# Loads and DMA transposes of an attention-plus-MLP kernel taken two pairs at a time and held apart

## The chip, the cores and the metric

One NeuronCore of a Trainium2 chip. The metric is the device time of one execution in microseconds (us), the median of several; most executions of the kernel before agree within 0.3%. A profile is one execution; its span is some 1.7 to 2.8 us shorter than the time of the same execution, since the time includes what lies before the first and after the last instruction.

## The reference, cut to what matters

```python
# q, k, v: (4 batches, 8 heads, 768 steps, 64) float32
for t in range(S):
    state = gamma * state + outer(k_t, v_t)          # per batch and head
    y_t   = scale * q_t @ state
x = y as (3072 tokens, 512)
h = x @ w_in                                         # 512 -> 2048
out = (h * cos(h)) @ w_out                           # 2048 -> 512
```

The kernel does the recurrence in chunks of 128 steps. A **pair** is one chunk of two batches: its q, k, v are 6 x 256 KB, and there are 12 pairs (0 to 11). A **group** is two pairs, 512 tokens of the MLP. "The fourth pair" is pair 3.

## The kernel before: the parts that matter

For every pair: load q, k, v (DMA); multiply q and v by decay factors and turn them into bf16 (`conv_q`, `conv_v`, mostly on POOL); turn k into bf16 (`conv_k`, on ACT); transpose q and k (`stage_t` on PE with an eviction by DVE, or `stage_t_dma`, a DMA transpose from SP); scores on PE and masking on DVE (`attend`); output and state (`stage_y`), whose result ACT copies into `xt`, the MLP's input. The MLP's first half is `unit_f` / `pair_f` (matmuls, cosine on ACT, product on DVE), its second half `unit_o`.

In these profiles each engine takes its instructions in the order in which the program emits them, and stands at the first one that isn't ready (below, ACT stands 2.33 us at the conversion of k5 with cosines behind it). POOL issues the loads, too. The stretch around pairs 3 to 6, cut:

```python
conv_k(3, True)                                      # ACT
conv_q(3, nc.gpsimd)                                 # POOL
load(nc.sync, 4, ("q0", "q1"))                       # SP issues, 256 KB each
load(nc.gpsimd, 4, ("k0", "k1", "v0", "v1"))         # POOL issues
conv_v(3, nc.gpsimd)
load(nc.sync, 5, ...); load(nc.gpsimd, 5, ...)
...
pair_f(2, 0)
stage_t(3, 0); stage_t(3, 1)                         # PE: 16 transposes, DVE: 2 evictions
pair_f(2, 1)
attend(3)
conv_q(4, nc.gpsimd); conv_v(4, nc.gpsimd); conv_k(4, True)
stage_t_dma(4)                                       # SP: DMA transposes, two a pair
load(nc.gpsimd, 6, ...)
pair_f(2, 2); pair_f(2, 3, (0,))
stage_y(3, nc.scalar.copy)                           # writes xt, which pair_f(3, .) reads
pair_f(2, 3, (1,))
conv_q(5, ...); conv_v(5, ...); load(nc.gpsimd, 7, ...)
pair_f(3, 0)
conv_k(5, True); stage_t_dma(5)
...
```

So loads of later pairs and transposes of earlier ones are in flight side by side. Source buffers are reused (`SLOT`), converted tiles have three copies (`NB = 3`).

## Time and profile before

| | before |
|---|---|
| time, median of 4 runs | 208.88 us (208.86 to 209.13) |
| span of the profiled run (a further one, of 209.35 us) | 207.6 us |
| PE busy | 199.5 us, 96% |
| POOL busy | 102.3 us, 49% (99.8% from 50 to 110 us) |
| DMA transposes, issue to landing | 2.7 / 4.6 / 13.8 us (least, median, most) |

The prediction shows how the page is read. Two more stretches of the timeline matter for what follows (columns: start, length, engine, line, what, count). POOL, which issues a load of 256 KB about every 0.88 us:

```profile
54.84 0.93 POOL L132 DMA_DIRECT2D qf<-in_q_dram  x1
55.77 0.88 POOL L132 DMA_DIRECT2D kf<-in_k_dram  x1
56.65 0.88 POOL L132 DMA_DIRECT2D qf<-in_q_dram  x1
57.52 0.88 POOL L132 DMA_DIRECT2D kf<-in_k_dram  x1
```

### The profile page before, as it was taken

How to read it: one execution, taken by the hardware profiler on the slowest of the kernel's cores; microseconds unless marked ns; L12 is line 12 of the kernel's file. 1: busy time of each engine (PE TensorE's matmuls, PEld its weight loads, DVE VectorE, ACT ScalarE, POOL GpSimd, SP SyncE). 2: the span in 40 equal slices, each digit the busy share in tenths (PEclk: the TensorE clock that was granted, in tenths of full speed). 3: DMA queues.
4: the chain of work that ended last, by engine and by line, in shares of the span. 5: the costliest groups of instructions: out<-in, count | busy, mean ns of one | idle time of the engine just before them, and what ended most of it. 6: DMA issues, size and time to landing. Idle time of an engine off the chain costs nothing.

```text
span 207.6 us, 4155 instructions
## 1 busy us (share of the span) xinstructions
PE 199.5 (96%) x1624; PEld 113.5 (55%) x1646; DVE 113.3 (55%) x188; ACT 114.1 (55%) x193; POOL 102.3 (49%) x118
## 2 busy tenths in 40 slices
PE   6889999999999999999999999999999999999993
PEld 1467554558997555546544465544465444444452
DVE  4691984554957454869874466854367244443000
ACT  6767872257996336577753754653554653553120
POOL 8999238399999999999995230000000000000000
PEclk9999999999999999999999999999999999999999
DMA  6999999999999999959799931141101100110222
GB/s 158 351 237 203 215 252 287 336 261 358 258 251 257 264 252 254 255 184 218 242 177 92 252 82 50 55 103 51 51 3 51 51 18 36 51 52 21 80 77 78
DMA packets 36644, 33.83 MB, mean 163 GB/s; under 512 B 26768, under 2 KB 29072, under 8 KB 36624
## 3 DMA queue, kind: packets, MB, share of 16 engines
q0 software_dynamic: 7808, 20.98, 39.4%
q1 hardware_dynamic: 27632, 12.23, 25.4%
q10 hardware_dynamic: 1184, 0.36, 0.7%
q8 instruction: 13, 0.21, 0.4%
q14 instruction: 7, 0.06, 0.1%
HBM read 27.26 MB, written 6.29 MB: 162 GB/s over the span
## 4 chain that ended last, share of the span: by engine, by line
PE 91%; DVE 4%; DMA 2%; issue 1%; DVEq 0%
PE bank L381 38%; PE bank L340 32%; PE bank L351 7%; PE bank L281 3%; PE bank L259 3%; PE bank L286 2%; DMA qf<-in_q_dram 2%; DVE am L268 2%; PE bank L398 2%; PE bank L232 1%; PE st_ps L303 1%; DVE qk L197 1%; DVE qkt L216 1%; PE bank L362 1%; PE bank L369 1%
## 5 line engine op out<-in xcount | busy, mean ns | idle before, releaser
L333 DVE TENSOR_TENSOR gt<-bank,cosb 128x512 bf16<-128x512 f32 x96 | 64.9, 689 | 61.9 <-ACT cosb L329 61.4
L329 ACT ACTIVATE cosb<-bank,halfpi 128x512 bf16<-128x512 f32 x96 | 65.1, 688 | 50.0 <-PE bank L340 44.4
L381 PE MATMUL bank<-w_out_sb,gt 128*128 128x512 bf16 x359 | 88.5, 379 | 0.7 <-issue 0.3
L340 PE MATMUL bank<-xt,w_in 128*128 128x512 bf16 x294 | 74.3, 380 | 0.7 <-issue 0.3
L381 PEld LDWEIGHTS <-gt 128*128 128x128 bf16 x368 | 35.5, 98 | 41.2
L340 PEld LDWEIGHTS <-w_in 128*128 128x128 bf16 x304 | 33.7, 114 | 30.9
L268 DVE TENSOR_TENSOR am<-bank,mask 128x512 bf16<-128x512 f32 x48 | 30.4, 682 | 3.9 <-PE bank L259 3.9
L388 ACT COPY ob<-bank 128x512 f32<-128x512 f32 x23 | 13.4, 586 | 18.4 <-PE bank L381 18.4
L204 POOL TENSOR_TENSOR vs<-vf,gk 128x512 bf16<-128x512 f32 x21 | 21.4, 1045 | 2.9 <-PE st_ps L303 2.9
L132 POOL DMA_DIRECT2D vf<-in_v_dram x23 | 20.3, 885 | 4.8 <-DMA w_out_sb<-in_moe_w_out_dram 4.8
L197 POOL TENSOR_TENSOR qk<-qf,gq 128x512 bf16<-128x512 f32 x18 | 18.5, 1051 | 7.8 <-issue 4.9
L132 POOL DMA_DIRECT2D kf<-in_k_dram x21 | 18.9, 901 | 1.8 <-DMA w_out_sb<-in_moe_w_out_dram 1.6
L210 ACT CAST qk<-kf 128x512 bf16<-128x512 f32 x24 | 13.9, 615 | 9.3 <-DMA kf<-in_k_dram 9.3
L290 ACT CAST xt<-bank 128x512 bf16<-128x512 f32 x24 | 12.9, 589 | 6.7 <-PE bank L286 6.7
L132 POOL DMA_DIRECT2D qf<-in_q_dram x18 | 16.2, 902 | 0.8 <-DMA w_in<-in_moe_w_in_dram 0.8
L351 PE MATMUL bank<-xt,w_in 128*128 128x256 bf16 x128 | 14.7, 273 | 0.0
L351 PEld LDWEIGHTS <-w_in 128*128 128x128 bf16 x128 | 13.8, 114 | 0.4
L286 PE MATMUL bank<-am,vs 128*64 128x128 bf16 x192 | 11.6, 220 | 0.0
L281 PEld LDWEIGHTS <-stb 128*64 128x64 bf16 x160 | 8.7, 109 | 4.3 <-issue 3.8
L281 PE MATMUL bank<-qkt,stb 128*64 128x128 bf16 x160 | 10.7, 222 | 0.3 <-DVE am L268 0.3
L286 PEld LDWEIGHTS <-vs 128*64 128x64 bf16 x192 | 9.9, 110 | 0.5 <-issue 0.4
L315 DVE CAST stb<-st_ps 64x512 bf16<-64x512 f32 x12 | 8.2, 685 | 2.7 <-PE st_ps L303 2.6
(46 smaller groups left out, 86.8 us busy)
## 6 DMA issues: line engine op xcount, KB each, us to landing
vf<-in_v_dram POOLq DMA_DIRECT2D x23, 256.0 KB, 5.8
out_dram<-ob SPq DMA_DIRECT2D x23, 256.0 KB, 2.0
kf<-in_k_dram POOLq DMA_DIRECT2D x21, 256.0 KB, 5.7
qf<-in_q_dram POOLq DMA_DIRECT2D x18, 256.0 KB, 5.3
w_out_sb<-in_moe_w_out_dram POOLq DMA_DIRECT2D x4, 512.0 KB, 12.5
qf<-in_q_dram SPq DMA_DIRECT2D x6, 256.0 KB, 8.1
w_in<-in_moe_w_in_dram POOLq DMA_DIRECT2D x3, 512.0 KB, 8.1
kf<-in_k_dram POOLq DMA_DIRECT2D x1, 512.0 KB, 5.4
```

The lines of the kernel that those rows point to most:

```text
L132: eng.dma_start(out=t[SLOT[p]][b], in_=src[2 * bp + b, :, ds(c * C, C)].rearrange("h t d -> t h d"))
L197: eng.tensor_tensor(out=qk[p % NB][:, b, 0], in0=qf[SLOT[p]][b], in1=bc(gq, p % NC), op=ALU.mult)
L204: eng.tensor_tensor(out=vs[p % NB][:, b], in0=vf[SLOT[p]][b], in1=bc(gk, p % NC), op=ALU.mult)
L210: nc.scalar.copy(out=qk[p % NB][:, b, 1], in_=kf[SLOT[p]][b])
L268: nc.vector.tensor_tensor(out=am[p % 2][b][j], in0=ap[j], in1=mask.unsqueeze(1).to_broadcast([128, HP, 128]), op=ALU.mult)
L281: nc.tensor.matmul(yp[ts(j, 64), a, :], lhsT=stb[p % 2][:, b, a, ts(j, 64)], rhs=qt(n, b, a), start=True, stop=False, skip_group_check=True)
L286: nc.tensor.matmul(yp[ts(j, 64), a, :], lhsT=vs[n][:, b, 2 * a + j, :], rhs=am[p % 2][b][j][:, a, :], start=(c == 0), stop=True, skip_grou ...
L329: nc.scalar.activation(out=cb, in_=bank, func=AF.Sin, bias=halfpi)
L333: nc.vector.tensor_tensor(out=out, in0=bank, in1=cb, op=ALU.mult)
L340: nc.tensor.matmul(bank, lhsT=w_in_t(i, f), rhs=xt[g % 2][:, i, :], start=(i == 0), stop=(i == KIN - 1))
L351: nc.tensor.matmul(bank[:, ts(e, 256)], lhsT=w_in_t(i, f + e), rhs=xt[g % 2][:, i, ts(hf, 256)], start=(i == 0 and e == 0), stop=(i == KIN ...
L381: nc.tensor.matmul(bank, lhsT=gt[g % 2][:, f, ts(j, 128)], rhs=w_out_sb[:, f, :], start=(f == 0), stop=(f == KOUT - 1))
```

## The change

The intent: take the fourth pair's transposes off PE, and from that pair on let the DMA do one kind of thing at a time, for two pairs: six loads of 512 KB (both batches in one transfer), then the transposes of both pairs. What holds the next loads back is a **gate**, a small copy on POOL that reads what the first of the last pair's two transposes writes: POOL can't issue the next loads before that one has landed. The core of the diff:

```diff
-    def load_k(p): ...
+    def load_both(*names):
+        for n, p in names:                       # one 512 KB transfer, both batches
+            bp, c = divmod(p, NC)
+            nc.gpsimd.dma_start(out=both[n][SLOT[p]]..., in_=SRC[n][1][2 * bp : 2 * bp + 2, ...])
...
+            conv_k(3, True)
-    conv_k(3, True)
-    conv_q(3, nc.gpsimd)
-    load(nc.sync, 4, ...) ; load(nc.gpsimd, 4, ...) ; conv_v(3, nc.gpsimd)
-    load(nc.sync, 5, ...) ; load(nc.gpsimd, 5, ...)
+    def turn(ps, loads=()):
+        for p in ps: conv_q(p, nc.gpsimd)
+        for p in sorted(ps): stage_t_dma(p)
+        for p in sorted(ps): conv_v(p, nc.gpsimd)
+        if loads:
+            nc.gpsimd.tensor_copy(out=gate, in_=qkt[max(ps) % NB][:, 0, 1, HP - 1, 126:])
+            load_both(k, q of the first, k, q of the second, v, v)
+    turn((3,), (4, 5))
...
     pair_f(2, 0)
-    stage_t(3, 0)
-    stage_t(3, 1)
+    conv_k(4, True)
     pair_f(2, 1)
     attend(3)
-    conv_q(4, ...) ; conv_v(4, ...) ; conv_k(4, True) ; stage_t_dma(4) ; load(nc.gpsimd, 6, ...)
+    conv_k(5, True)
+    turn((5, 4), (6, 7))
...  # the same for later pairs: turn((6, 7), (8, 9)), turn((8, 9), (10, 11)), turn((10,)), turn((11,))
```

`conv_k(4)` and `conv_k(5)` move forward on ACT, and the q product of pair 5 comes before that of pair 4. The conversions of later k are moved as well.

More of the change, by code (lines that the diff above doesn't have):

```diff
@@ L97 @@
     w_out_sb = sb([128, KOUT, DM], BF16, "w_out_sb")
-    qf = [[sb([128, H, D], FP32, f"qf{i}_{b}") for b in range(2)] for i in range(PRE)]
-    kf2 = [sb([128, 2, H, D], FP32, f"kf{i}") for i in range(PRE)]
-    kf = [[t[:, b] for b in range(2)] for t in kf2]
-    vf = [[sb([128, H, D], FP32, f"vf{i}_{b}") for b in range(2)] for i in range(PRE)]
+    both = {n: [sb([128, 2, H, D], FP32, f"{n}f{i}") for i in range(PRE)] for n in "qkv"}
+    qf, kf, vf = [[[t[:, b] for b in range(2)] for t in both[n]] for n in "qkv"]
     ob = [sb([128, DM], FP32, f"ob{i}") for i in range(4)]
@@ L120 @@
     rel = sb([128, 128], FP32, "rel")
+    gate = sb([128, 2], BF16, "gate")
     SRC = {"q": (qf, q), "k": (kf, k), "v": (vf, v)}
@@ L134, in load @@
                 in_=src[2 * bp + b, :, ds(c * C, C)].rearrange("h t d -> t h d"))
-    def load_k(p):
-        bp, c = divmod(p, NC)
-        nc.gpsimd.dma_start(
-            out=kf2[SLOT[p]].rearrange("p b h d -> p (b h) d"),
-            in_=k[2 * bp : 2 * bp + 2, :, ds(c * C, C)].rearrange("b h t d -> t (b h) d"))
+    def load_both(*names):
+        for n, p in names:
+            bp, c = divmod(p, NC)
+            nc.gpsimd.dma_start(
+                out=both[n][SLOT[p]].rearrange("p b h d -> p (b h) d"),
+                in_=SRC[n][1][2 * bp : 2 * bp + 2, :, ds(c * C, C)].rearrange(
+                    "b h t d -> t (b h) d"))
     def load_w_in(r):
@@ L171 @@
     load(nc.gpsimd, 1, ("q1",))
-    load_k(1)
+    load_both(("k", 1))
     load(nc.gpsimd, 0, ("v0", "v1"))
@@ L493 @@
             conv_v(2, nc.vector, (1,))
+            conv_k(3, True)
         elif u == 11:
             stage_m(2, stage_a(2, 1))
-    conv_k(3, True)
-    conv_q(3, nc.gpsimd)
-    load(nc.sync, 4, ("q0", "q1"))
-    load(nc.gpsimd, 4, ("k0", "k1", "v0", "v1"))
-    conv_v(3, nc.gpsimd)
-    load(nc.sync, 5, ("q0", "q1", "v0"))
-    load(nc.gpsimd, 5, ("k0", "k1", "v1"))
+    def turn(ps, loads=()):
+        for p in ps:
+            conv_q(p, nc.gpsimd)
+        for p in sorted(ps):
+            stage_t_dma(p)
+        for p in sorted(ps):
+            conv_v(p, nc.gpsimd)
+        if loads:
+            nc.gpsimd.tensor_copy(out=gate, in_=qkt[max(ps) % NB][:, 0, 1, HP - 1, 126:])
+            load_both(*[(n, p) for n, p in (
+                ("k", 0), ("q", 0), ("k", 1), ("q", 1), ("v", 0), ("v", 1)) for p in [loads[p]]])
+    turn((3,), (4, 5))
     for j in range(4):
@@ L507 @@
     pair_f(2, 0)
-    stage_t(3, 0)
-    stage_t(3, 1)
+    conv_k(4, True)
     pair_f(2, 1)
     attend(3)
-    conv_q(4, nc.gpsimd)
-    conv_v(4, nc.gpsimd)
-    conv_k(4, True)
-    stage_t_dma(4)
-    load(nc.gpsimd, 6, ("q0", "k0", "q1", "k1", "v0", "v1"))
+    conv_k(5, True)
+    turn((5, 4), (6, 7))
     pair_f(2, 2)
@@ L520 @@
     pair_f(2, 3, (1,))
-    conv_q(5, nc.gpsimd)
-    conv_v(5, nc.gpsimd)
-    load(nc.gpsimd, 7, ("q0", "k0", "q1", "k1", "v0", "v1"))
     pair_f(3, 0)
-    conv_k(5, True)
-    stage_t_dma(5)
     pair_f(3, 1)
     pair_f(3, 2)
-    conv_q(6, nc.gpsimd)
-    conv_k(6, True)
-    conv_v(6, nc.gpsimd)
     pair_f(3, 3)
-    def ahead(p):
-        if p < NP:
-            conv_q(p, nc.gpsimd)
-            conv_k(p, True)
-            conv_v(p, nc.gpsimd)
-    def fetch(p):
-        load(nc.gpsimd, p, ("q0", "k0", "q1", "k1", "v0", "v1"))
-    def later(p):
-        stage_y(p)
-        n = 8 if p == 4 else p + 3 if p > 5 else NP
-        if n < NP:
-            fetch(n)
     late = []
@@ L568 @@
     attend(4)
-    stage_t_dma(6)
     o_units(1, 2, 6)
-    later(4)
+    conv_k(6, True)
+    stage_y(4)
     attend(5)
+    conv_k(7, True)
+    turn((6, 7), (8, 9))
     o_units(1, 6, 10)
-    later(5)
+    stage_y(5)
+    k_at = {(2, 6): 8, (2, 9): 9, (3, 2): 10, (3, 12): 11}
+    t_at = {(2, 9): ((8, 9), (10, 11)), (3, 3): ((10,),), (3, 13): ((11,),)}
+    a_at = {(2, 2): 6, (2, 10): 7, (3, 2): 8}
+    y_at = {(2, 6): 6, (2, 14): 7, (4, 14): 11}
     for g in range(2, NG + 1):
         for s in range(16):
-            hf, r = divmod(s, 8)
-            p = 2 * (g + 1) + hf
             if g == 2 and s % 2 == 0 and s < 12:
@@ L588 @@
                     last_o(g - 1, 3)
-            while late and late[0][0] <= 16 * g + s:
+            now = 16 * g + s
+            while late and late[0][0] <= now:
                 late.pop(0)[1]()
-            if p < NP:
-                if r == 0:
-                    ahead(p + 1)
-                elif r == 1:
-                    if p + 1 < NP:
-                        stage_t_dma(p + 1)
-                elif r == 2 and p in (6, 7, 8):
-                    todo = [stage_a(p, b) for b in range(2)]
-                    stage_m(p, todo[0])
-                    put_off(16 * g + s + 1, lambda todo=todo, p=p: stage_m(p, todo[1]))
-                elif r == 6 and p in (6, 7, 11):
-                    later(p)
-                elif (g, s) == (3, 4):
-                    fetch(11)
-                if (g, s) in joined:
-                    join(joined[g, s], 16 * g + s)
+            at = (g, s)
+            if at in k_at:
+                conv_k(k_at[at], True)
+            if at in t_at:
+                turn(*t_at[at])
+            if at in a_at:
+                p = a_at[at]
+                todo = [stage_a(p, b) for b in range(2)]
+                stage_m(p, todo[0])
+                put_off(now + 1, lambda todo=todo, p=p: stage_m(p, todo[1]))
+            if at in y_at:
+                stage_y(y_at[at])
+            if at in joined:
+                join(joined[at], now)
 _INS = ['q', 'k', 'v', 'moe_w_in', 'moe_w_out']
```

## The prediction

> **What bounds the kernel now.** I read the page first: busy shares, then the chain of work that ended last.
>
> ```profile
> PE 199.5 (96%) x1624; PEld 113.5 (55%) x1646; DVE 113.3 (55%) x188; ACT 114.1 (55%) x193; POOL 102.3 (49%) x118
> ...
> PE 91%; DVE 4%; DMA 2%; issue 1%; DVEq 0%
> ```
>
> TensorE is busy nearly all the time, and 91% of the chain is its own work. A busy PE need not be at its peak, so I looked at its timeline for stalls. From 16.7 us (first MLP matmul) to 204.1 us the PE never stops: four 512-column matmuls take 0.86 us in the chain (0.216 us each), and the same 0.86 stands in a row of pieces to the end. The work inside these 187.4 us adds up as follows. MLP: 768 matmuls of 512 columns (or the same columns in halves) x 0.216 = 165.9. Attention of pairs 2 to 11, by the start-to-start times in the timeline: 10 score blocks of 0.55, 10 output blocks of about 0.9, 8 state blocks of 0.35, 2 transposes of a pair at 0.89: about 19. Together some 185, so 2 to 3 us are left for changes of kind (0.1 each) and small gaps. There is no large wait to take away. The stretch that the change touches on PE is this (start, length, group):
>
> ```profile
> 47.48 1.91 PE L351 MATMUL bank<-xt,w_in 128*128 128x256 bf16 x16
> 49.23 1.06 PE L232 MATMUL bank<-ident,qk 128*128 128x128 bf16 x16
> 50.12 1.91 PE L351 MATMUL bank<-xt,w_in 128*128 128x256 bf16 x16
> 51.96 0.62 PE L259 MATMUL bank<-qkt 64*128 64x128 bf16 x16
> 52.52 2.81 PE L351 MATMUL bank<-xt,w_in 128*128 128x256 bf16 x24
> 55.26 0.25 PE L281 MATMUL bank<-qkt,stb 128*64 128x128 bf16 x2
> ```
>
> The 16 transposes (line 232) of the fourth pair stand between two blocks of pair_f; then come its scores (259), 1.5 blocks of pair_f, and its output (281). What feeds the output is the masking on DVE (268), which stands behind the evictions of those transposes (216) and two gt products (333); in front of the products stands ACT:
>
> ```profile
> 50.82 1.28 DVE L216 TENSOR_SCALAR qkt<-bank 128x512 uint32<-128x512 uint32 x2
> 52.01 1.47 DVE L333 TENSOR_TENSOR gt<-bank,cosb 128x512 bf16<-128x512 f32 x2
> 53.40 2.48 DVE L268 TENSOR_TENSOR am<-bank,mask 128x512 bf16<-128x512 f32 x4
> ...
> 49.49 0.69 ACT L329 ACTIVATE cosb<-bank,halfpi 128x512 bf16<-128x512 f32 x1 [0.20 <-PE bank L351]
> 51.26 1.50 ACT L329 ACTIVATE cosb<-bank,halfpi 128x512 bf16<-128x512 f32 x2 [1.08 <-PE bank L351]
> 52.66 1.13 ACT L210 CAST qk<-kf 128x512 bf16<-128x512 f32 x2
> ```
>
> The masks end at 55.88 and PE's output of the fourth pair, started at 55.26, ends at about 56.3. So PE is only just not waiting for DVE here. That is the place where the change can lose what it wins.
>
> **The DMA side.** It is full until about 110 us, but nothing on PE waits for it after the start. The queues:
>
> ```profile
> q0 software_dynamic: 7808, 20.98, 39.4%
> q1 hardware_dynamic: 27632, 12.23, 25.4%
> ...
> DMA to landing us min/median/max: 2.7/4.6/13.8
> ```
>
> The third line is that of the transposed tiles, issue to landing: 2.7 us in the quiet, 13.8 us at the worst, at about 104 us, where a whole pair of loads and an output stand beside it. POOL, which issues the loads at 0.88 us each and does the q and v products at 1.05 each, is 99.8% busy from 50 to 110 us.
>
> **What the Trainium skill says.** (1) "DMA: Bandwidth & Descriptors", section "Queues, rings and completion order": each DMA engine goes round robin among the queue rows at packet granularity. The trace agrees with the consequence: POOL's packets have 20.98 MB / 7808 = 2.7 KB on average, those of the hardware queue 443 B, so a transpose beside POOL's loads gets a small share and is slow. (2) The same page, "Rules for kernel authors": a transpose next to ordinary DMAs "needs nothing". So holding them apart is for time, not for correctness. (3) The same page, "Anatomy of one DMA", fits 2.0 us + bytes / 436 GB/s. That would be 2.6 us for 256 KB; the trace has 5.3 to 5.8 as the median of its loads under contention and 3.8 to 4.2 in the quieter ones. The measured ones are used.
>
> **The change, part by part.**
> 1. Fourth pair's transposes by DMA: PE loses 16 matmuls. From 47.48 to 51.96 are 4.48 us; two blocks of 16 half-width matmuls at 0.109 and a change of kind are 3.56. Gain on PE: 0.9 us. DVE loses two evictions, 1.28 us. The transposes can go at about 41.0 and 42.7 (the products of q end there on POOL, 39.95 + 1.04 and 41.6 + 1.04) and land at about 45 and 46, well before the scores at about 51.
> 2. Loads of pairs 4 and 5 no longer leave at 42 to 50 us (and partly earlier by SP, whose q4 and q5 loads fall away), but after the gate, which waits for the fourth pair's first transpose and stands behind its v products: 42.64 + 2.05 = 44.7, or the landing at 45. I take 45. Six loads of 512 KB, each issued in 1.15 us (the one such load in the page's row for kf took 1.151 us). First landing: 1.15 + some 2.2 + 512 KB at 320 GB/s (landings of pair 3's loads are 0.82 us apart per 256 KB) = 5 us, so k4 at 50, then 1.65 us apart: q4 51.7, k5 53.4, q5 55, v4 56.7, v5 58.3. The four outputs at 44 to 49 us (1 MB) can push k5 to 54 or 55.
> 3. ACT: the conversion of k4 moves ahead of the two cosines of the second pair_f. It starts when k4 lands, at 50.1, ends at 51.2; cosines end at 52.4; gt products at 53.3; four masks at 53.3 to 55.8. PE, 0.9 us earlier, would want to do the fourth pair's output from 54.3 to 55.3, and has to wait: it ends at about 56.2, as before. **So DVE's saved evictions and PE's saved transposes are nearly given back to k4's conversion; 0.1 to 0.3 us are left of 0.9.** Each microsecond by which k4 lands after 50.1 is lost outright.
> 4. Then ACT converts k5, wanted at 52.4, landing at 53.4 to 55: the three cosines after it and the xt copies of the fourth pair come at 56.3 to 57.5 instead of 57.1; the next pair_f needs them at about 57.4. Loss 0 to 1.5 us.
> 5. The turns. Pairs 4 and 5: q products from 55 to 59.2, transposes issued at 58.2, 59.4, 60.7, 62 (1.27 each), T(4) landed at about 62.5, wanted at 65.5. Second gate at 63.6; k6 68.6, k7 71.9, wanted by ACT at 69.5 and 72.3. T(6) lands by 77.5, wanted at 81. Third gate at 79.7; k8 at 84.8, wanted at 86. From there the distance grows. No PE wait, with 1 to 4 us to spare.
> 6. POOL: 36 loads of 0.88 for pairs 6 to 11 (31.7 us), and the part of pairs 4 and 5's that POOL issued, become 24 of 1.15 (27.6 us) for pairs 4 to 11; the gates, about 0.1 each, are nothing. POOL is no longer full, but was not what PE waited for.
>
> Sum: -0.9 + 0.7 (step 3) + 0 to 1.5 (step 4, taken as 0.3, since the schedule looks tuned for it) = about -0.1. Prediction 208.8 us.
>
> **Rivals.** (a) All of the 0.9 us is kept: the first loads land a microsecond earlier than I reckon, because the DMA is empty at the gate. For it: the DMA is indeed left alone with outputs. Against: ACT's and DVE's order, which holds the masks back whatever lands. Time 208.0. (b) The gate starves ACT: first transposes land late (4.6 median, not 4), outputs take their share, k4 and k5 land 2 us late; ACT is in order, so cosines, masks and xt copies wait, and PE runs dry. Time 210 to 211. (c) The later turns fail too: one load in two turns lands late and a transposed pair is not there when PE wants it; 2 to 4 us more each time, 212 to 215. The margins of 3 to 4 us on T speak against it; the 1.2 us for k8 and 0.4 to 0.9 for k6 and k7 are thin, though ACT has idle time there. (d) Transposes apart from loads speed up the later part: they do, but no engine that ends the kernel waits for them. No gain.
>
> **Range and chances.** The floor is 208.9 - 0.9 = 208.0, and nothing else is on offer; with noise 207.8. Rival (b) reaches 211. Over 2% faster would be under 204.7, which no step gives: 1%. Over 2% slower is above 213.1, which takes (c): 4%.
>
> **What would show each step right or wrong.** No line of transposes on PE at 49 us and no evictions on DVE at 51; k4's conversion on ACT starting at about 50 with a wait for the DMA before it, k5's at 53 to 55; masks of the fourth pair ending near 55.8 (step 3), its output on PE ending near 56.2; a small hole on PE before the next pair_f (step 4). Transposes landing in about 3 us each; gates on POOL near 45, 63.6 and 79.7. If PE has waits before scores of pairs 4 to 7, rival (c) holds. The prediction is wrong if the masks end by 55 (then rival a), or if the loads after the gate land later than 55 (then b).

## More of the kernel before

PE at the scores of pair 6: no wait stands before them (an idle time of the engine would be printed in brackets at the end of the line).

```profile
80.34 1.03 PE L340 MATMUL bank<-xt,w_in 128*128 128x512 bf16 x4
81.30 0.62 PE L259 MATMUL bank<-qkt 64*128 64x128 bf16 x16
81.85 1.05 PE L340 MATMUL bank<-xt,w_in 128*128 128x512 bf16 x4
```

## The result, and the profile after

| | before | after |
|---|---|---|
| time, median of 4 runs | 208.88 us | 212.55 us (212.41 to 212.78) |
| span of the profiled run | 207.6 us | 210.7 us |
| PE busy | 199.5 us | 198.9 us |
| POOL busy | 102.3 us | 93.3 us |
| DMA transposes to landing | 2.7 / 4.6 / 13.8 | 2.7 / 3.2 / 7.6 |

The ratio is 1.0174, with a 95% interval of 1.0156 to 1.0192. Ratios here are not quite the quotient of the medians. Executions over 1.5% slower than the fastest of the same kernel are left out of the means. Within the 2% that counts as the same, but 1.55 us beyond the top of my range.

PE does 0.6 us less, as intended, and the kernel is 3.7 us longer. So PE waits. The busy line and the shares of the chain that ended last:

```profile
PE 198.9 (94%) x1608; PEld 112.8 (54%) x1630; DVE 112.5 (53%) x186; ACT 114.4 (54%) x193; POOL 93.3 (44%) x103
...
PE 75%; DMA 9%; DVE 7%; issue 3%; ACT 3%; POOL 2%; DVEq 0%; ACTq 0%; POOLq 0%
```

The chain was 91% PE before. Now a quarter of it belongs to others, 5% to the transposes alone. PE's timeline says where it idles; these are its pieces with a wait of more than 0.2 us in brackets, from 50 to 86 us:

```profile
52.95 1.91 PE L352 MATMUL bank<-xt,w_in 128*128 128x256 bf16 x16 [0.65 <-DVE gt L334]
55.95 0.22 PE L287 MATMUL bank<-am,vs 128*64 128x128 bf16 x1 [0.38 <-DVE am L269]
58.98 7.15 PE L352 MATMUL bank<-xt,w_in 128*128 128x256 bf16 x64 [1.24 <-ACT xt L291]
84.69 0.40 PE L260 MATMUL bank<-qkt 64*128 64x128 bf16 x8 [1.58 <-DMA qkt<-qk]
```

To see what they add up to, I compare the starts of the same work in both profiles. The profiled run after began its MLP 0.38 us earlier than that of before, ahead of any changed instruction on PE (some of PE's first work, four transposes near 6.5 us among it, took longer in the profile before), so the last column adds 0.38.

| work on PE | before | after | difference | aligned |
|---|---|---|---|---|
| `pair_f(2, 0)` | 47.48 | 47.10 | -0.38 | 0 |
| scores of pair 3 | 51.96 | 50.69 | -1.27 | **-0.89** |
| output of pair 3 | 55.26 | 54.79 | -0.47 | -0.09 |
| the half block of pair_f behind it | 56.66 | 56.68 | +0.02 | **+0.40** |
| first MLP output of group 1 | 64.55 | 65.96 | +1.41 | **+1.79** |
| first scores of pair 6 | 81.30 | 82.71 | +1.41 | +1.79 |
| `unit_f` behind them | 81.85 | 85.02 | +3.17 | **+3.55** |
| last output unit | 200.43 | 203.88 | +3.45 | +3.83 |

The 0.9 us of transposes are won, and then lost in three steps: 1.3 us between pair 3's scores and the end of its output, 1.4 us at `pair_f(3, 0)`, 1.8 us at pair 6's scores. Each has a load or transpose behind it. ACT around the first two:

```profile
50.45 1.14 ACT L211 CAST qk<-kf 128x512 bf16<-128x512 f32 x2 [0.65 <-DMA kf<-in_k_dram]
51.50 1.26 ACT L330 ACTIVATE cosb<-bank,halfpi 128x512 bf16<-128x512 f32 x2
55.09 1.14 ACT L211 CAST qk<-kf 128x512 bf16<-128x512 f32 x2 [2.33 <-DMA kf<-in_k_dram]
56.13 1.84 ACT L330 ACTIVATE cosb<-bank,halfpi 128x512 bf16<-128x512 f32 x3
57.85 1.08 ACT L291 CAST xt<-bank 128x512 bf16<-128x512 f32 x2
```

ACT waits for k4 and k5, and cosines and the xt copies, which were ready to go, stand behind those conversions. For the third step, the chain in order of time (start, length, what), followed back from pair 6's scores:

```profile
63.23 2.74 DMA qkt<-qk
66.02 0.08 issue
66.10 0.19 POOL gate L506
66.28 0.43 issue
66.72 1.19 POOL kf L138
67.91 1.15 POOL qf L138
69.06 1.13 POOL kf L138
70.19 5.43 DMA qf<-in_q_dram
75.62 1.00 POOL qk L198
76.62 0.43 issue
77.05 7.59 DMA qkt<-qk
```

Read it downwards: pair 5's first transpose lands at 66.0, the gate opens, loads of 6 and 7 are issued, their q arrives, POOL multiplies it, the second transpose of pair 6 leaves at 77.05 and takes 7.59 us. (The chain's links are inferred. The q load issued at 70.19 is pair 7's and landed only at 78.19; pair 6's, issued at 67.91, landed at 74.51 and is the one that these products need.) What the DMA queues carried in two stretches of that flight, 77.5 to 78.5 us and 79.5 to 80.5 us (packets, MB, share of the 16 engines' time; q0 is the queue of POOL's loads, q1 that of the transposes):

```profile
q0 software_dynamic: 94, 0.34, 101.7%
...
q1 hardware_dynamic: 384, 0.10, 90.4%
q0 software_dynamic: 40, 0.11, 34.8%
```

In the first of these windows not one packet of the transposes moved, though the issue of pair 6's first had ended at 76.89 and that of the second was under way; they ran as the loads ran out. The transposes of pairs 3, 4 and 5, with at most the first or last of some loads beside them, landed in 2.7 to 2.8 us each. So the change holds transposes apart from the *next* turn's loads, but not from the rest of their own: pair 6's left while q7, v6 and v7 were still coming.

Pairs 4 and 5 escaped this by the order of their q products, and paid for it. q4 had landed at 53.05, but POOL stood until q5 came:

```profile
57.34 4.04 POOL L198 TENSOR_TENSOR qk<-qf,gq 128x512 bf16<-128x512 f32 x4 [5.49 <-DMA qf<-in_q_dram]
```

With pair 4's products first, POOL's work alone would have let the second gate open at about 63.4 in place of 66.1 (57.3 + 2.0 for pair 5's q + 4.1 for the v products; an estimate from this trace). But pair 4's transposes would then have left beside loads. **No run tests this order**, so how much of the loss it is stays open.

### The profile page after: what moved, and what is told of

It reads as the page before. It is cut to its first block, busy times and chain, and to the rows that moved or that the text cites. A ratio compares the mean times of both kernels' runs of the same rounds, so it can differ in the third digit from the quotient of the medians.

```text
span 210.7 us, 4083 instructions
## 1 busy us (share of the span) xinstructions
PE 198.9 (94%) x1608; PEld 112.8 (54%) x1630; DVE 112.5 (53%) x186; ACT 114.4 (54%) x193; POOL 93.3 (44%) x103
## 4 chain that ended last, share of the span: by engine, by line
PE 75%; DMA 9%; DVE 7%; issue 3%; ACT 3%; POOL 2%; DVEq 0%; ACTq 0%; POOLq 0%
PE bank L382 33%; PE bank L341 28%; DMA qkt<-qk 5%; DMA qf<-in_q_dram 4%; DVE am L269 4%; PE bank L352 3%; PE bank L282 2%; PE bank L260 2%; PE bank L287 2%; PE bank L399 2%; ACT cosb L330 2%; DVE qkt L217 1%; POOL kf L138 1%; DVE gt L334 1%; DVE qk L198 1%
## 5 line engine op out<-in xcount | busy, mean ns | idle before, releaser
L352 PEld LDWEIGHTS <-w_in 128*128 128x128 bf16 x128 | 13.8, 113 | 2.6 <-issue 2.2
L138 POOL DMA_DIRECT2D kf<-in_k_dram x9 | 10.5, 1169 | 1.2 <-issue 0.8
L260 PE MATMUL bank<-qkt 64*128 64x128 bf16 x192 | 8.1, 218 | 2.8 <-DMA qkt<-qk 1.6
L260 PEld LDWEIGHTS <-qkt 64*128 64x128 bf16 x192 | 5.4, 94 | 7.2 <-DVE qkt L217 2.5
```

The source lines that it names most:

```text
L260: nc.tensor.matmul(ap[j][:, a, :], lhsT=kt(n, b, a)[po : po + 64, :], rhs=qt(n, b, a)[po : po + 64, :], tile_position=(po, 0))
L352: nc.tensor.matmul(bank[:, ts(e, 256)], lhsT=w_in_t(i, f + e), rhs=xt[g % 2][:, i, ts(hf, 256)], start=(i == 0 and e == 0), stop=(i == KIN ...
```

## The experiments

**Theory A**, formed after this reading: from the first gate on, loads, q product, transposes, gate and next loads make a serial chain on DMA and POOL (gates at 44.8, 66.1, 85.7: some 20 us for two pairs), and the landing of pair 6's second transpose, where PE meets it, sets the time from 85 us on. **Theory B**: the gates as such. **Theory C**: PE's holes are independent and add up. Later a fourth came in: the **merging** of the loads. All runs stand beside runs of the kernel before on the same chip.

### The gates away (`no_gate`)

```diff
-            nc.gpsimd.tensor_copy(out=gate, in_=qkt[max(ps) % NB][:, 0, 1, HP - 1, 126:])
```

> The changed kernel without its four gates on POOL. The gate before pair 4's loads was never waited for in the trace (POOL reached it at 44.81 and it took 0.18 us); the second held POOL 0.69 + 0.43 us, the third 1.3 + 0.4. Theory A (the serial chain loads -> q product -> transpose -> gate -> loads paces the kernel, and the transpose of pair 6 that lands last is its end): loads of 6 and 7 start some 1.3 us earlier, the hole of 1.58 us before pair 6's second scores shrinks to about 0.3, time 211.2. Theory B (the gates are the cause and without them all is as good as before): 208.9 or less. Theory C (two holes of equal standing, the one at 58 us of pair_f and the one at 84 us): the hole at 58 us stays 1.2 us, time 211.2 as in A.

Measured: 211.93 us (211.03 to 212.50), ratio 1.0127. In the profiled run, the slowest of the five, no wait stands before pair 6's scores any more, but PE comes to them 1.4 us later (84.12 for 82.71): the holes before 60 us are there, and longer (1.11, 0.38, 1.71). So the gates cost 0.6 us by the medians and 1.0 by the ratios (0.0047 of 209 us), not 3.7: theory B alone falls.

### k4's and k5's conversions late, mis-built and mended (`k_late`, `k_late2`)

> The changed kernel with the conversions of k4 and k5 on ACT put back where the kernel before had them (after pair 3's scores, and after the first pair_f of pair 3). The waits at 50.5 and 55.1 us on ACT then come after what PE needs. Theory C (the holes add up): the 0.65 + 0.38 + 1.24 us of holes at 52 to 59 us go, PE is 2.2 us earlier, time 210.2. Theory A (the landing of pair 6's second transpose, which hangs on DMA and POOL alone, sets the time): PE comes 2.2 us earlier to the same landing at 84.6, the hole there grows from 1.6 to about 3.8, and the time stays 212.4 to 212.6.

This kernel gave a wrong result (relative error 0.22), and its 217.5 us say nothing: I had left pair 5's transpose ahead of k5's conversion in the program, so it transposed old data. Mended:

```diff
     pair_f(2, 1)
     attend(3)
-    conv_k(5, True)
-    turn((5, 4), (6, 7))
+    conv_k(4, True)           # was ahead of pair_f(2, 1)
 ...
     pair_f(3, 0)
+    conv_k(5, True)
+    turn((5, 4), (6, 7))
```

> The earlier run k_late was mis-built: pair 5's transpose was put ahead of k5's conversion, so it transposed old data, and the conversion waited for it. Here the turn of pairs 4 and 5 is moved behind k5's conversion too (POOL and SP have nothing in between, so their order is unchanged). Theory C (holes add up): the holes of 0.65 + 0.38 + 1.24 us at 52 to 59 us go, PE is some 2.2 us earlier, time 210.3. Theory A (the landing of pair 6's second transpose sets the time from 84.7 us on): that hole grows from 1.6 to about 3.8 us and the time stays 212.3 to 212.6.

Measured: 211.90 us (210.37 to 213.06), ratio 1.0137. Between the two: all the holes before 60 us are gone, worth 2.2 us by theory C, and the median gains 0.65, which is not clear of noise (the interval of this ratio, 1.0104 to 1.0170, overlaps the changed kernel's). The profiled run, the fastest with 210.37, has one large wait left, a new one, in front of `unit_f`:

```profile
78.57 1.89 PE L341 MATMUL bank<-xt,w_in 128*128 128x512 bf16 x8 [1.90 <-ACT xt L291]
```

ACT waited there for k7's conversion, which stands ahead of the xt copies of pair 5. PE came earlier and met the next link of the same chain: the holes are not independent. The spread of 2.7 us says that this end of the chain varies from run to run, and I can't say by which link.

### Pair 6's flight without v6 and v7 (`no_v67`)

```diff
                 ("k", 0), ("q", 0), ("k", 1), ("q", 1), ("v", 0), ("v", 1)) for p in [loads[p]]
+                if not (n == "v" and p in (6, 7))])
```

> The changed kernel without the loads of v for pairs 6 and 7 (wrong result on purpose). It asks whether pair 6's second transpose took 7.6 us because v6 and v7 were in flight beside it. Theory A: it lands in about 3.5 to 4 us instead of 7.6, that is at about 81, the hole at 84 us is gone, time 210.9 (the hole at 58 us still there). If transposes are slow for another reason, it lands at 84 still and the time is 212.5.

Measured: 211.37 us (211.16 to 211.59), ratio 1.0116, with the wrong result that was meant. Pair 6's transposes landed in 3.6 and 3.1 us in place of 6.6 and 7.6, pair 7's in 3.4 and 2.7 in place of 4.2 and 2.9, and PE ran through pair 6's scores:

```profile
82.73 0.62 PE L260 MATMUL bank<-qkt 64*128 64x128 bf16 x16
```

So the slowness of that flight is the loads beside it, and 1.2 us of the loss is this. The holes before 60 us stayed (0.78, 0.38, 1.17).

### Slack: more work on PE, more work on the chain (`pe_delay`, `chain_delay`)

```diff
+    for _ in range(7): nc.tensor.matmul(extra, ...)        # pe_delay, before o_units(1, 0, 2); attend(4)
```

> The changed kernel with seven matmuls that nobody reads (512 columns, 7 x 0.216 = 1.5 us) put on PE just before pair 4's scores, at 65.9 us. If PE's own work set the time from 59 us on, the time rises by the whole 1.5 us, to 214.0. Theory A (from 84.7 us on the time hangs on the landing of pair 6's transposes, which come from the chain of loads, q products, transposes and gate): PE only reaches the same landing with a smaller hole; the hole of 1.58 us shrinks to about 0.1 and the time stays 212.5 to 212.8.

Measured: 212.80 us (212.57 to 213.03), ratio 1.0176 where the changed kernel has 1.0174. **1.5 us of work were added to PE and 0.25 us came out.** (By the ratios it is 0.04.) In its profile the wait before pair 6's scores is gone; PE arrives at 84.86:

```profile
84.86 0.62 PE L260 MATMUL bank<-qkt 64*128 64x128 bf16 x16
```

This is the clearest run of all: at that point PE's own work does not set the time.

```diff
+        if loads and max(ps) == 5:                           # chain_delay
+            conv_v(5, nc.gpsimd)                             # a second time
```

> The changed kernel with pair 5's v products done twice on POOL (2 x 1.04 = 2.1 us more) ahead of the second gate; nothing else. Theory A: this is on the chain, less the 0.69 us that POOL waited at that gate, so the loads of 6 and 7 go 1.4 us later and everything behind: 212.5 + 1.4 = 213.9. If POOL and the loads have slack there, the time stays 212.5.

Measured: 213.49 us (213.15 to 213.87), ratio 1.0210. The second gate came at 67.07 us, 0.97 later than in the changed kernel, and the time rose by 0.94. I had expected 1.4; the profile shows that this run's q products began 0.28 us earlier. What arrived at the gate came out at the end, nearly one for one (0.75 us by the ratios).

### Pair 6's transposes on PE (`k_late_t6pe`)

```diff
-            stage_t_dma(p)
+            if p != 6: stage_t_dma(p)                        # and stage_t(6, .) at (2, 1)
```

(with the edit of `k_late2`)

> As k_late2, and pair 6's transposes by PE as the fourth pair's were before (16 matmuls, two evictions), so nothing on PE waits for pair 6's transfer. Theory A: both holes are gone, 1.0 us of transposes comes back: 212.5 - 2.2 - 1.6 + 1.0 = 209.7, close to the kernel before, with pair 7's landing as the next thing to wait for. If the time stays above 211, another wait that I have not named follows behind.

Measured: 211.88 us (211.21 to 212.30), ratio 1.0136: no better than `k_late2`. A miss, and it names the wait I had not: PE idles 2.19 us for the xt copies of pair 5, at 79.36, since ACT stands at k7's conversion from 73.7 to 76.7. In the changed kernel k7's load is issued at 69.05 and takes 7.4 us, landing at 76.41; I had reckoned 71.9. Taking away one end of the chain uncovers the next.

### The transfers unmerged (`halves`)

```diff
+            if p > 3:
+                load(nc.gpsimd, p, (n + "0", n + "1"))
+                continue
```

> The changed kernel with each of the 512 KB loads as two of 256 KB (12 issues of 0.88 us a turn in place of 6 of 1.15). A rival says that the merged transfers are late because each lands only as a whole. If so, k5's first half lands earlier than 55.1 and the hole at 58 us shrinks, time under 212. Theory A: bandwidth and the chain set it; issuing 10.6 us in place of 6.9 makes it no better, time 212.5 to 214.

Measured: 211.22 us (210.28 to 212.45), ratio 1.0111. My expectation was wrong: **splitting is worth 1.3 us.** The reason is argued, not shown: issued at 0.88 us per 256 KB, the loads come hardly faster than the DMA moves them; at 1.15 us per 512 KB they would pile up ahead of it, and the transposes stand behind the pile. With halves, pair 6's and 7's landed in 3.4 us in the median, with no wait on PE for them; pair 6's second left 1.7 us later than in the changed kernel and landed 2.0 us earlier. The rival in the expectation, that a merged load lands only as a whole, isn't told apart by this run. k5 still lands late (a hole of 0.71 before `pair_f(3, 0)`, behind holes of 1.19 and 0.38 at pair 3).

### Two edits together (`no_gate_klate`, `halves_klate`)

The first is the edit of `no_gate` with that of `k_late2`, the second the edit of `halves` with that of `k_late2`.

> Both mending edits together: no gates, and k4's and k5's conversions late as in k_late2. Each alone gave about 0.6 us. Theory A: without the holes at 52 to 59 us PE comes earlier to the waits on pairs 6 and 7, which the missing gate moves earlier by about 1 us only: 210.5 to 211.5, still slower than the kernel before. If the holes were independent: 209.5 or less.

Measured: 210.73 us over six runs, one of them slow at 214.20, ratio 1.0073. As theory A has it: two edits of 0.6 us each, 1.8 together, and PE still waits before 83 us (0.87 for xt, 0.84 and 0.33 for pair 6's transposes).

> The changed kernel with 256 KB loads (as in halves) and k4's and k5's conversions late (as in k_late2). If merging and the early conversions are all that is wrong, both holes are gone and the 0.9 us of PE work are won: 208.0 to 208.5. If the serial turns (loads, then transposes, then the next loads) are too long by themselves, PE now waits for k7's conversion or pair 6's transposes: 209.5 to 210.5.

Measured: 210.94 us (210.30 to 213.12), ratio 1.0104. With merging and early conversions both undone, the median is still 2 us behind the kernel before. The profiled run (211.75) has waits of 0.44 and 1.00 for xt copies and of 0.52 and 0.51 for pair 6's transposes. So what is left of the change, the serial turns with their gates and the order of q products in them, is still too long; this run doesn't separate these.

### One part alone in the kernel before (`b_t3dma`, `b_merged`)

```diff
 # b_t3dma, on the kernel before
     load(nc.sync, 4, ("q0", "q1"))
+    stage_t_dma(3)
 ...
-    stage_t(3, 0)
-    stage_t(3, 1)
```

> The kernel before with one part of the change alone: the fourth pair's transposes by DMA, issued on SP between q4's and q5's loads; loads, order and conversions as before. Expected: 16 matmuls less on PE, 0.9 us, and the masks no longer late because the conversion of k4 stays behind the cosines: 208.0. If the transposes, beside pair 4's loads, land after 51 us, PE waits for them and the time is 209 to 211.

The fourth pair's transposes by DMA with all else as before: one run at 209.16 us, five from 223 to 257. The profile of a slow run shows that the fourth pair's own transposes landed in time (4.4 and 6.4 us) and that everything later didn't: loads issued between 55 and 89 us took 8 to 19 us and transposes 9 to 26, with PE waiting up to 6.3 us before scores. Only slow runs show this, and why one placement on SP sets it off stays open. `hybrid`, below, has the same transposes by DMA with the loads of pairs 4 and 5 merged and held behind them, and all six of its runs took 208.61 to 209.75.

```diff
 # b_merged, on the kernel before; the same for pairs 7 to 11
-    load(nc.gpsimd, 6, ("q0", "k0", "q1", "k1", "v0", "v1"))
+    load_both(("q", 6), ("k", 6), ("v", 6))
```

> The kernel before with the loads of pairs 6 to 11 merged to 512 KB, nothing else (transposes of the fourth pair on PE, loads and transposes overlapped). POOL gains 1.8 us a pair. If merged loads build a backlog in the DMA queues that slows the transposes beside them, their landings grow from 4.6 us in the median to 7 or more; PE waits only where more than 5 us of slack are used up: 208.9 to 209.5. If merging is harmless the landings stay and the time is 208.9.

Measured, fast runs: 208.84 to 209.16, ratio 1.0002. Merging the loads of pairs 6 to 11 alone costs nothing in those. The profiled run was a slow one (211.98): transposes took 7.2 us in the median and 14.6 at most, and PE waited 2.45 us at pair 8's scores. That the landings are as long in the fast runs I can't show.

### Toward a version that beats both (`hybrid`, `hybrid2`, `hybrid3`, `hybrid4`)

The first keeps what the change wins, pair 3's transposes by DMA, held apart, and goes back to the old order from pair 4 on.

```diff
-    load(nc.sync, 4, ...); load(nc.gpsimd, 4, ...); conv_v(3, ...); load(nc.sync, 5, ...); load(nc.gpsimd, 5, ...)
+    stage_t_dma(3)
+    conv_v(3, nc.gpsimd)
+    nc.gpsimd.tensor_copy(out=gate, in_=qkt[0][:, 0, 1, HP - 1, 126:])
+    load_both(("k", 4), ("q", 4), ("v", 4), ("k", 5), ("q", 5), ("v", 5))
 ...
-    stage_t(3, 0); stage_t(3, 1)
```

> Made to beat both: the kernel before, with the fourth pair's transposes by DMA and pairs 4 and 5's loads held behind them by the gate (merged, pair 4's k, q, v first), conversions of k and everything from pair 4's q product on as before, with loads and transposes overlapped. If theory A is right the loss is in the later turns and in k's early conversions, and the 0.9 us of PE work are won: 208.0. If the late start of pair 4 and 5's loads costs by itself, POOL's work is 2 to 3 us later and waits appear at pair 5's or 6's scores: 209 or more.

Measured: 209.32 us (208.61 to 209.75), ratio 1.0007 (0.9994 to 1.0021): the same as before. Its profile keeps the gain up to 65 us and loses it to k6's conversion on ACT. `hybrid2` puts that conversion later:

```diff
     conv_q(6, nc.gpsimd)
-    conv_k(6, True)
 ...
-    stage_t_dma(6)
     o_units(1, 2, 6)
+    conv_k(6, True)
+    stage_t_dma(6)
```

> The hybrid with its one remaining fault mended: k6's conversion stood on ACT ahead of the last two cosines of pair 3 and waited for k6 (2.2 + 0.9 us), so cosines, gt products and pair 4's masks came late and PE lost 0.4 us and more at pair 4's output. Here it stands after the next two output units, where the changed kernel has it, and pair 6's transposes behind it. Expected: the gain of 0.9 us at the fourth pair is kept but for 0.3 us at pair 4's second scores: 208.3. If pair 6's scores now wait for its transposes, 209 again.

Measured: 208.86 us, ratio 0.9998 (0.9954 to 1.0042), in two levels: 207.92, 207.92 and 208.10 in three runs, 209.62 to 210.85 in the other three. At the lower level the 0.9 us are there, and PE has no wait over 0.2 us. I then tried twice to remove the upper level. `hybrid3` splits the loads and puts q products ahead of the next loads; `hybrid4` holds pair 6's loads behind pair 4's transposes by a second gate.

```diff
 # hybrid3, on hybrid2; load_both also as in halves, and conv_v(4) moved to just ahead of the load of 6
-    load(nc.gpsimd, 6, ...)                  # was ahead of conv_q(5)
     conv_q(5, nc.gpsimd)
+    load(nc.gpsimd, 6, ...)
     conv_v(5, nc.gpsimd)
-    load(nc.gpsimd, 7, ...)
 ...
     conv_q(6, nc.gpsimd)
+    load(nc.gpsimd, 7, ...)
 # hybrid4, on hybrid2; loads of 7 merged
-    load(nc.gpsimd, 6, ...)                  # was ahead of conv_q(5)
     conv_q(5, nc.gpsimd)
+    nc.gpsimd.tensor_copy(out=gate, in_=qkt[1][:, 1, 1, HP - 1, 126:])
+    load(nc.gpsimd, 6, ...)
```

> hybrid2 with 256 KB loads and another order on POOL: the q products of pairs 4 and 5 ahead of pair 6's loads, pair 6's q product ahead of pair 7's loads, so that pair 4's, 5's and 6's transposes mostly find no backlog of loads. Expected: no hole on PE, 208.0, and all runs within 0.5 us of each other. If the slow level of hybrid2 has another cause, some runs are at 209.6 and more again.

> hybrid2 with pair 5's q product ahead of pair 6's loads, a second gate (pair 4's last transpose has landed) before pair 6's loads, and pair 7's loads merged to make up for the time on POOL. Pair 4's transposes then stand beside pair 5's loads only, pair 5's beside little. If their landing makes the second level of hybrid2, all runs are at 207.9 to 208.3. If the runs still spread to 209.6 and more, the second level has another cause, or pair 6's k and transposes are late in their turn.

Measured: 212.46 us and 214.52 us, each with two slow runs among six (fast runs of `hybrid3` 209.83 to 212.57, ratio 1.0128; of `hybrid4` 213.25 to 214.68, ratio 1.0248). The only profile of `hybrid3` is of a slow run (214.02): there ACT waited for k7, whose load I had moved, 1.87 and 1.58 us in front of a cosine, and PE idled 3.44 us. My order may have been bad and not the idea; that isn't shown. In `hybrid4` the gate opened only at 63.28, because pair 4's transposes still stood behind pair 5's loads, and pair 6's transposes were late by 1.19 and 2.08 us. In `hybrid4`, then, what held the loads back on POOL was paid for at pair 6's scores. What makes the upper level of `hybrid2` stays open, since its only profile is of the lower. No version here is reliably faster than the kernel before.

## Why the prediction was wrong, point by point

- **What bounds the kernel, and the gain on PE**: right. 0.89 us less, aligned, at pair 3's scores; the chain of before was PE's own work.
- **Part 1, pair 3's transposes**: right. Issued from 40.92 us, landed in 2.8 us each (I had 4), no wait for them.
- **Part 2, the gate at 45 and first landings**: the gate opened at 44.8. k4's conversion began at 50.45 for 50.1; k5's at 55.09, the far end of "53.4 to 55"; q5's product at 57.34 for 55. The term that was mis-sized is the spacing of the landings, 1.65 us per 512 KB. From k4 (44.94 + 5.5 = 50.4) to the last v (9.5 us after its issue at about 50.7, so 60.2) it is 9.8 us for five, 2.0 each.
- **Part 3, the gain given back at k4's conversion**: the mechanism was right and the size too small. I expected 0.6 to 0.8 us back; 1.3 came back, 0.40 us worse than before in place of 0.1 to 0.3 better. I had missed that pair_f would also wait for a PSUM bank (0.65 us for a gt product).
- **Part 4, k5 and the xt copies**: the mechanism was right, range "0 to 1.5 us"; it was 1.4. I took 0.3 into the sum "since the schedule looks tuned for it", which is not a number from a profile.
- **Part 5, "No PE wait, with 1 to 4 us to spare"**: this is the step that failed. The second gate came at 66.10 for 63.6, k6's conversion at 73.02 for a landing at 68.6, k7 at 76.41 for 71.9, and pair 6's second transpose at 84.6 for 77.5. I moved each time forward with the figures of the first turn, so its 2 us were missed again in the second. Part 5 gives pair 4's and 5's transposes some 3 us of flight (59.4 to 62.5, 60.7 to 63.6), which is what they had, and nothing longer is said for pair 6's, though I had myself written that a transpose beside POOL's loads is slow. Its flight was 7.59. `no_v67` shows the loads as its cause, `pe_delay` and `chain_delay` that this chain, not PE, sets the time.
- **Part 6, POOL's load**: right (93.3 us for 102.3, not the bound by its busy time), and misleading: POOL was freer and yet later, because it waited.
- **The sum**: as written, -0.9 + 0.7 + 0.3 is +0.1 and not -0.1, so 209.0 by its own terms; a slip of 0.2 us that decides nothing. The issues of transposes, "1.27 each", are 1.40 to 1.41 us apart in the trace of the kernel before (61.26 to 62.66, 70.57 to 71.98).
- **The rivals**: (b) and (c) together are what happened, to which I gave 4% above the 2% line and a top of 211. The two holes are not simply their sum: `pe_delay` and `k_late2` show that time lost before 80 us is partly hidden by the wait at pair 6. My sentence "no engine that ends the kernel waits for them", on the speed of later transposes, was the wrong one: PE did.
- **What is not settled**: how the 3.7 us divide among merging (1.3 by the medians), gates (0.6), conversions (0.65) and serial turns (some 2 left with the first and third undone), in which the order of the q products of pairs 4 and 5 is an untested part. These don't add, since each uncovers the next wait, and several of these kernels spread by 2 to 3 us from run to run.

## What to carry to other kernels

Before holding two kinds of transfer apart, write down the whole loop that this makes serial and its length against the pace at which the bound engine uses up its product; here about 20 us per two pairs, on a PE that in the kernel before asked for pair 6's transposes 15 us after pair 4's (scores at 66.4 and 81.3). From pair 6 to pair 8 it is 23.5 us (81.3 to 104.8), and the changed kernel has no wait over 0.2 us after 85. Put a conversion that waits for a load behind the work of the same in-order engine that others wait for. And test a suspected wait from both sides: work added to the bound engine that doesn't show (1.5 us in, 0.25 out) tells more than any hole in its timeline.

## What the Trainium skill lacked or had wrong

- "DMA: Bandwidth & Descriptors", section "Rules for kernel authors", says a transpose beside ordinary DMAs "needs nothing". For correctness no run here contradicts it. It lacks what the neighbours cost in time: 2.7 us alone, 7.59 us beside the last three 512 KB loads of a turn, 13.8 us at most in the kernel before.
- The same page, section "Queues, rings and completion order", has each DMA engine go round robin among its queues by packet. In the changed kernel from 77.5 to 78.5 us the loads' queue moved 94 packets and the transposes' none, though the issue of one transpose had ended at 76.89; their first packets came after 79.1. Whether descriptors were late (the issue of the second took 4.15 us, 1.24 in the quiet) or the arbitration passed them over, the trace doesn't show.
- The same page, in "Rules for kernel authors", asks for 1 MiB or more per DMA for bandwidth, and to join many small transfers. No page says that larger transfers can cost time where transposes follow them: going from 512 KB back to 256 KB made the changed kernel 1.3 us faster (212.55 to 211.22).
- The same page's fit in "Anatomy of one DMA", 2.0 us + bytes / 436 GB/s, gives an estimate of 3.2 us for 512 KB. The shortest of the 512 KB loads after a gate took 5.0 us from the start of its issue to landing, k4's 5.5 and the later ones of a turn 5.6 to 9.5; in a chain of transfers the measured ones are to be used.
